# High parts of 16 weight pieces cast by transfers of GpSimd instead of by ScalarE, in a kernel whose issue order was searched anew

## The chip, the cores and the metric

The kernel runs on one core of one Trainium2 chip. The metric is device time in microseconds (us); lower is better. PE is TensorE, DVE is VectorE, ACT is ScalarE, POOL is GpSimd, SP is SyncE, which here only issues transfers. SPq, ACTq and POOLq are the queues from which these engines issue them.

## The reference, cut to what matters

Two parts follow each other: a linear recurrence with complex decay over 768 steps of 32 heads, and a gated feed-forward block on its output, with float32 weights.

```python
for t in range(S):                       # attention: 4 batches x 8 heads, D = 48
    S_re, S_im = ar*S_re - ai*S_im + k_t v_t^T, ar*S_im + ai*S_re
    y[t] = q_t @ S_re
x = y.transpose(0, 2, 1, 3).reshape(3072, 384)
h = x @ w_in                             # 384 x 2048
sp = log1p(exp(h))
out = (h * tanh(sp)) @ w_out             # 2048 x 384
```

## The kernel before

The tokens are cut into 12 units of 256 (`UNITS`, named u0 to u11), each into two chunks a and b of 128. Each unit goes through three stages. `elementwise(u)` turns the decays into phases and growth factors on ACT and DVE and rotates q and k ("turn sin", "turn cos"); SP then copies the results into the tile `T` ("relay", line 566, six transfers per chunk), with the heads side by side. `attention(u)` is a set of small matmuls per chunk: `kn` (transpose of the keys), `am` (scores), `y` (output) and `pd` (state). `moe(u)` takes the outputs as `x`, split into a high part `xH` and a rest `xL`, through eight pairs p0 to p7 of weight blocks: "mm1" (`ph`, line 787), a chain of five operations on ACT and DVE up to `g`, its high part `gh` and rest `gl`, and "mm2" (`po`, line 824). Only unit 0 multiplies the weights as they are; all others use a high part `wh` and a rest `wl` of each weight, so that a product takes three matmuls.

The weights arrive as 64-bit words, in 16 pieces w0 to w15 (even ones are of w_in, odd ones of w_out). `weight(i)` makes float32 of a piece by four instructions (low, shift, join, carry); `halves(i)` then writes the high part (line 318, "high") and the rest (line 323, "rest", on DVE, which reads both `w` and `wh`).

Nothing schedules at run time. Every step is recorded by `op(...)` with the engines that may do it, and `Work.issue` emits the 2446 steps in the order of the table `ORDER`; a letter behind a number picks another engine than the first of the step's list (V is DVE, A is ACT, G is POOL, S is SP). Each engine then works through its own instructions in that order. Forty steps "spin" (line 886, two matmuls each that nobody reads) lie in the order of PE's start. POOL clears one column of the tile `kn` (line 628) for each chunk that passes on its state.

The program ends with a verdict on the inputs: "tally" (DVE) counts flags of all units, "tally sum" (PE) adds them over partitions, "judge" (DVE, line 899) writes `okay`. Every engine reads `okay` at the end of its own order (line 933) and branches; behind the branch ACT scales the last half of unit 11 (line 835) and SP stores it (line 841). The first half is stored by POOL.

Of the kernel before, what the change touches and what calls it, by code (L numbers as in the profile page):

```python
# [55 lines left out]
72 0 1 73 127 3 74 2 75 128 7V 5 8 76 10V 4 9 11 77 6 12 192 78 13 202 197 14 79 24V 80 27V 81 82 25 83 169V 15 19 28  # L56
26 132V 84 16 166V 85 133 22 17 86 167 23 87 31 170 88 32 135V 18 134 34 33 29 137 89 21 136 90 20 91 42 47 46G 45 92
35 48 30 49 93 43 36 44 194 50 193 53 52 94 139 39 95 54 195 96 55 97 40 51 98 37 196V 99 38 100 56A 60 207 101 62A
140 562 102 204 57 563 103 203V 104 199 105 41 200 106 61A 138 107 58 64 108 142 109 59 205 112 66 116 67A 68 113 118
65A 117 70 71A 114 206V 123 69 198 110 119 217 141 120 124 115V 121 201V 125 430 63 143 209 212 126 567 208V 210 144  # L60
122 146 186 211V 145 130 168 153 570V 147A 185 173 171 149 148 568 184 151 111 218V 187 174 155 154 571G 360A 129 175
150V 160 152 156 222 157 432 219 569 158 220 356 163 573 161 164 214 159 221V 273 172 189 357 215 188 213 272 191 162
176 216V 361A 190 358 177 359 227 274 165 363 178 575 275 365 367 276 364 223 224 282 366 572 181A 368 277 225 283 369
576 232 182 179 370 226V 278 292 131 180 229 237 284 279 293 376A 371 183 230 280 374 228 578 574 281 285 231V 372
375A 286 303 378 242 373 287 233V 386 234 388 362 583 302 235 387 382 389 390 288 236V 294 392 434 289 247 383 295 304
312 584 296 385 238 239 379 290 391 381A 384 393 297 380 291 240 442 743 305 243 395 377 244 577 241V 394 298 245 252
306 397 744 400 307 246V 398 446 299 401 257 248 579 322 396 399 308 402 249 403 448 405 580 313 749 404 250 406 323
314 581 251V 407 582 315 262 309 409 316 564 585 408 594A 317 565 300 593 586 324 253 254 301 436 410 431 318 411 263
255 412 258 325 264 414 326 256V 415 587A 417 265 450 267 418 413 332 266V 327 421 259 440 420 433 310 328 566 588 452
423 333 422 438 319 260 343 334 329 589 335 320 592 321 590 428V 595 435 336 311 591 596 426 424 330 337 429 597 603  # L70
342 602 598 338 331 425 344 604 427 268 269 601 339 463 750 747 345 609 270 346 462 607 752 261V 419 347 456 599 271V
348 474 751 754G 605 475 476 437 340 349 935 341 606 439 608 350 477 454 464 444 351 478 753 416 441 757 612 610 613
354 355 352 479 755 465 611V 466 487 616 614 600 443 758 617 619 445 467 621 480 468 615 618 760 481 623 469 624 936
622 470 759 761 625 756 765 486 498 447 499 626 628 510 511 488 489 471 472 473 458 500 501 762 944 490 620 629 482A
# [12 lines left out]
975 842 859 860 849 991 1147 1148 1156 824 1157 989 1155 843A 976 1159A 992 726 1315 737 738 1130 1129 739 740 850 851
1160G 872 990 1158 996 1161 741 1162 998 997 993 1001 1165 1316 871 852 844 1318V 999 845 1002 861 1169 1172 1003 1317
1499 862 1320 1007 994 1000 1004 1008 853 1166 1005 995V 863 864 865 846 1006 1014 1322 866 867A 1015 854 1010 855 873
1319G 1321 1323 1163 1167 1171 1009 1012 1168 1011V 1013 874 875 1016 1164 856 1331 742 868 883 876 877 1324 1332 878  # L90
884 885 1325 1333 1018 1334A 895 896 897 886 887 888 1170 1500 1020 889 857 1326 858 1019 1335 879 880 898 1505 899
890 907 1327 869 870 1017 1021 900 891 1178 892 1023V 1022 1024 1025V 1026 881 908 901 902 1336 1508 1179 1176 1177
882 919 1328 1314 1173 920 1132 909 1506 1131 910 903A 921 1330 904 911 922 1509 912 1511 1329 1342G 1182 1180 1183
1181 923 913 924 1507 914 925 893 1174 894 1175 915 1513 1027 1028 1312 1338V 905 906 1510 1029 926 1187 1341G 1189
1190 1188 1191G 916 1185 1184 1311 1340 1337 1344 1192 1030 1345 1194 1512 1521 1339 1351 1040 1039 1041 927 928 1051
1349 1031 1352 1032 1357 1042 1193 1186V 1052 1033 1034 1195 1522 1043 1044 1045 1046 917 918 929 930 1523 1524 1035A
1053 1514 1355 1054 1347 1036 1196 1516 1197 1198 1202 1199 1201 1047A 933 931V 934 1064 1055 1056 1057 1048 1350 1200
1075 1063 1065 1066 932 1076 1037 1038 1049 1058 1059 1060 1343 1353 1354 1515 1050 1087 1067 1088 1068 1077 1069 1070
# [12 lines left out]
1287 1288 1400 1886 1895 1289 1694 1693 1722 1290 1567 1724 1719 1401 1402 1568V 1896 1565 1721 1726 1733 1412 1729
1403 1404 1405 1406 1411 1407 1735 1413 1424 1414 1291 1725 1423 1425 1426 1292 1303 1304 1566V 1557 1569 1570 1305
# [101 lines left out]
def tile_kernel(ctx, tc, q, k, v, vs, are, aim, are_t, aim_t, w_in, w_out, out):  # L214
    nc = tc.nc
# [8 lines left out]
    op = Work(nc)  # L224
# [83 lines left out]
    def halves(i):  # L308
        def high(e):
# [805 lines left out]
```

## Time and profile before

| what | value |
|---|---|
| time, median of 3 runs (least to most) | 581.17 us (580.46 to 581.74) |
| time of the profiled execution | 580.87 us |
| its span in the profile | 579.2 us |
| PE busy | 566.4 us, 98% |
| DVE busy | 486.1 us, 84% |
| ACT busy | 476.2 us, 82% |
| POOL busy | 27.4 us, 5% |

The span is the time between the first and the last instruction of the program; 1.67 us of the profiled execution's time lie outside it. Busy shares are means over the whole span: the kernel's start, its stage of weight unpacking (up to about 160 us), its long stage of steady work and its end differ much, and are read apart. The ends of matmuls are modelled by the profiler, so that PE looks busy also in short waits.

### The profile page before, as it was taken

What the parts mean: (1) busy time and instruction counts of PE and PEld (TensorE: products, weight loads), DVE (VectorE), ACT (ScalarE), POOL (GpSimd) and SP (SyncE); (2) the same over time, 40 slices, a digit from 0 to 9 for tenths busy, and PEclk for the clock granted to TensorE, in tenths of its full rate; (3) what the DMA queues carried; (4) which work ended last, traced back from release to release, by engine and by line L of the source; (5) the groups of instructions that cost most, each with busy time, mean ns of one, the idle gap of its engine ahead of it and who ended that gap; (6) DMA issues with size and microseconds to landing.
All of it is one profiled execution on the core that took longest, in us unless ns stands there. A gap on an engine that the chain in (4) does not pass through costs nothing.

```text
span 579.2 us, 13318 instructions
## 1 busy us (share of the span) xinstructions
PE 566.4 (98%) x5262; PEld 532.2 (92%) x5262; DVE 486.1 (84%) x899; ACT 476.2 (82%) x763; POOL 27.4 (5%) x59
## 2 busy tenths in 40 slices
PE   7999999999999999999999999999999999999994
PEld 4689788899999999999999999999999999999994
DVE  5999999999999999989899977999697857555462
ACT  7899999999999999888888978778778866456670
POOL 2010000110000010100000000200000000000000
PEclk9999999999999999999999999999999999999998
DMA  8788785512727155152352162064254230010201
GB/s 284 246 274 271 239 256 151 167 28 60 220 61 205 57 143 164 47 153 78 103 134 80 43 201 74 21 194 132 56 137 137 58 109 1 29 29 2 81 1 33
DMA packets 58469, 68.91 MB, mean 119 GB/s; under 512 B 4976, under 2 KB 51440, under 8 KB 58400
## 3 DMA queue, kind: packets, MB, share of 16 engines
q1 hardware_dynamic: 57616, 67.14, 39.0%
q8 instruction: 43, 0.70, 0.5%
q10 hardware_dynamic: 720, 0.66, 0.4%
q14 instruction: 26, 0.21, 0.1%
q0 software_dynamic: 64, 0.20, 0.1%
HBM read 39.52 MB, written 4.72 MB: 76 GB/s over the span
## 4 chain that ended last, share of the span: by engine, by line
PE 77%; ACT 10%; DVE 9%; issue 2%; POOL 1%; ACTq 0%; DVEq 0%; POOLq 0%
PE po L824 32%; PE ph L787 32%; PE ypsum L674 5%; PE pa L644 4%; ACT X L174 4%; PE pd L689 2%; ACT e L174 2%; PE pkn L622 2%; ACT L172 2%; DVE X L559 1%; DVE w L296 1%; DVE QK L535 1%; DVE g L800 1%; DVE wl L323 1%; ACT words L174 1%
## 5 line engine op out<-in xcount | busy, mean ns | idle before, releaser
L174 ACT ACTIVATE e<-e 128x512 f32<-128x512 f32 x192 | 119.6, 629 | 29.9 <-DVE e L856 27.8
L787 PE MATMUL ph<-xH,wh 128*128 128x256 f32 x462 | 132.8, 287 | 0.0
L787 PE MATMUL ph<-xH,wl 128*128 128x256 f32 x462 | 129.9, 281 | 0.0
L787 PE MATMUL ph<-xL,wh 128*128 128x256 f32 x462 | 129.8, 281 | 0.0
L824 PE MATMUL po<-wh,gh 128*128 128x384 f32 x308 | 105.1, 341 | 0.0
L824 PE MATMUL po<-wh,gl 128*128 128x384 f32 x308 | 103.5, 336 | 0.4 <-DVE gl L812 0.4
L824 PE MATMUL po<-wl,gh 128*128 128x384 f32 x308 | 103.5, 336 | 0.0
L800 DVE SCALAR_TENSOR_TENSOR g<-e,ph 128x512 f32<-128x512 f32 x96 | 65.3, 681 | 30.1 <-ACT e L174 29.2
L787 PEld LDWEIGHTS ph<-xH,wh 128*128 128x128 f32 x462 | 87.0, 188 | 1.7 <-issue 0.7
L787 PEld LDWEIGHTS ph<-xL,wh 128*128 128x128 f32 x462 | 87.0, 188 | 0.1
L787 PEld LDWEIGHTS ph<-xH,wl 128*128 128x128 f32 x462 | 87.0, 188 | 0.0
L174 ACT ACTIVATE e<-ph 128x512 f32<-128x512 f32 x96 | 56.8, 592 | 26.6 <-PE ph L787 24.0
L174 ACT ACTIVATE e<-e,fifth 128x512 f32<-128x512 f32 x96 | 69.3, 723 | 1.9
L812 DVE TENSOR_TENSOR gl<-g,gh 128x512 fp32r<-128x512 f32 x88 | 60.2, 685 | 6.3 <-PE po L824 2.3
L824 PEld LDWEIGHTS po<-wh,gh 128*128 128x128 f32 x308 | 57.9, 188 | 0.9 <-issue 0.2
L824 PEld LDWEIGHTS po<-wh,gl 128*128 128x128 f32 x308 | 57.9, 188 | 0.8 <-DVE gl L812 0.7
L824 PEld LDWEIGHTS po<-wl,gh 128*128 128x128 f32 x308 | 57.9, 188 | 0.0
L856 DVE TENSOR_SCALAR e<-e 128x512 f32<-128x512 f32 x96 | 44.1, 462 | 15.2 <-ACT e L174 14.8
L172 ACT ACT_TABLE_LOAD x40 | 51.3, 1283 | 0.7
L659 DVE TENSOR_TENSOR kept<-pa,cmask 64x128 f32<-64x128 f32 (+1 forms) x108 | 32.6, 329 | 11.5 <-PE pa L644 6.3
L674 PE MATMUL ypsum<-T,S 96*48 96x128 f32 x320 | 33.9, 276 | 0.0
L806 ACT CAST gh<-g 128x512 fp32r<-128x512 f32 x38 | 23.4, 617 | 12.2 <-DVE g L800 12.1
(145 smaller groups left out, 1120.1 us busy)
## 6 DMA issues: line engine op xcount, KB each, us to landing
T<-QK SPq DMA_DIRECT2D x70, 129.0 KB, 2.5
T<-X SPq DMA_DIRECT2D x69, 129.0 KB, 2.6
words<-w_in SPq DMA_DIRECT2D x8, 768.0 KB, 5.5
words<-w_out SPq DMA_DIRECT2D x8, 768.0 KB, 6.0
QK<-k SPq DMA_DIRECT2D x12, 384.0 KB, 4.3
QK<-q SPq DMA_DIRECT2D x12, 384.0 KB, 5.2
V<-v SPq DMA_DIRECT2D x12, 384.0 KB, 4.6
R<-a_re SPq DMA_DIRECT2D x12, 384.0 KB, 4.3
```

Of the source, the lines that this page charges most:

```text
L172: self.nc.scalar.preload_act_table_set(need)
L174: return self.nc.scalar.activation(out, in_, func, **kw)
L622: e.transpose(d["pkn", g][:, i, :], T()[:, 4 * g + i, 1, :C], ident)
L644: e.matmul(d["pa", g][r0:r0 + C // 2, i, k0:], T()[:, 4 * g + i, 1, k0:k0 + C // 2], T()[:, 4 * g + i, 0, k0:C], start=True, stop=True)
L659: e.tensor_tensor(x[r, :, two, t], y[r, :, two, t], m[r, :, two, t], ALU.mult)
L674: e.matmul(ypsum[64 * par:64 * par + D, i, :], lhs, rhs, start=m == 0, stop=first or m == 1)
L787: e.matmul(ph[k][:, slot(k, j, a), :], win(x, j, kt, a), st[y][:, kt, cols(k)], start=n == 0, stop=n + 1 == len(todo))
L800: e.scalar_tensor_tensor(g_[k], e_[k], 2.5, ph[k], ALU.subtract, ALU.mult)
L806: (e.copy if e is nc.scalar else e.tensor_copy)(gs[k][0], g_[k])
L812: e.tensor_tensor(gs[k][1], g_[k], gs[k][0].bitcast(F32), ALU.subtract)
L824: e.matmul(po[t], x[:, slot(k, j, a), 0 if halved else t * P:C if halved else (t + 1) * P], wout(y, j, a), start=j == 0 and a == 0 and n == 0,
L856: op("V", f"{n} cap", lambda e, k=k: e.tensor_scalar_min(e_[k], e_[k], math.exp(20.0)))
```

## The change

The step "high" of the 16 weight pieces may now only go to POOL, and is there a transfer from `w` to `wh` that casts on its way. Before, all 16 were casts on ACT. No relay is issued by ACT any more (five were). The table `ORDER` is another one from its first entry on; 49 of the steps that DVE did have gone to ACT (eight of them in the first 130 us: three kn copies and one step each of size, low, ends, xH and gh), 26 of those that ACT did have gone to DVE (none of them in those 130 us). ACT loads its function tables 43 times in place of 41. The same matmuls are issued, the spins among them. Of the diff the code stands here in full, and of the table one line of each side.

```diff
-72 0 1 73 127 3 74 2 75 128 7V 5 8 76 10V 4 9 11 77 6 12 192 78 13 202 197 14 79 24V 80 27V 81 82 25 83 169V 15 19 28
...
+0 7V 8 9 1 10V 12 11 72 73 74 13 75 76 77 78 79 80 81 82 83 84 14 127 85 132V 3 2 128 166V 24V 25 27V 192 15 133 135V
...
-            (e.copy if e is nc.scalar else e.tensor_copy)(wh[i], w[i])
+            e.dma_start(wh[i], w[i])
...
-        op("AV", f"w{i} high", high)
+        op("G", f"w{i} high", high)
```

Three places of the new order follow, each before and after.

POOL's order in the first 100 us before. `kn` is the column that is cleared per chunk, line 479 an addition of unit 2, line 480 a multiplication of unit 3.

```order
L541 COPY QK_140<-X_138 128x6
L628 MEMSET kn_352 128x8
L479 TENSOR_TENSOR X_427<-X_427 128x6x128
L628 MEMSET kn_488 128x8
L628 MEMSET kn_713 128x8
L628 MEMSET kn_871 128x8
L480 TENSOR_TENSOR I_806<-I_806,X1_1091 128x768
```

The same place after; `wh` is the pair of high parts that a transfer writes, `w` the piece that it reads.

```order
L541 COPY QK_207<-X_121 128x6
L628 MEMSET kn_349 128x8
L318 DMA wh_369<-w_297 128x768
L628 MEMSET kn_458 128x8
L318 DMA wh_533<-w_486 128x768
L479 TENSOR_TENSOR X_413<-X_413 128x6x128
L318 DMA wh_369<-w_410 128x768
L318 DMA wh_645<-w_580 128x768
L318 DMA wh_645<-w_647 128x768
L318 DMA wh_679<-w_205 128x768
L628 MEMSET kn_699 128x8
```

Sixteen such transfers stand on POOL's queue, among clearings and additions that wait for other engines; the last is issued before POOL's addition of unit 4.

SP's order at the relays of unit 0 before: `T_264` is chunk a, `T_343` chunk b; ACT issues what is missing (one of chunk a, three of chunk b).

```order
L566 DMA T_264<-X_138 16x8x258 x2
L566 DMA T_264<-QK_140 16x8x258 x2
L566 DMA T_264<-X_138 16x8x258
L282 DMA words_296<-w_out 128x768
L381 DMA R_302<-a_re 128x768
L381 DMA I_310<-a_im 128x768
L566 DMA T_343<-X_138 16x8x258
L566 DMA T_343<-QK_140 16x8x258 x2
```

SP's order there after: `T_293` is chunk a, `T_332` chunk b.

```order
L388 DMA QK_207<-k 128x6x128
L282 DMA words_233<-w_out 128x768
L381 DMA R_259<-a_re 128x768
L381 DMA I_261<-a_im 128x768
L393 DMA V_265<-v 128x768
L566 DMA T_293<-X_121 16x8x258 x3
L566 DMA T_293<-QK_207 16x8x258 x3
L282 DMA words_320<-w_out 128x768
L566 DMA T_332<-X_121 16x8x258 x3
L566 DMA T_332<-QK_207 16x8x258 x3
```

All twelve relays now stand on one queue, and the first two loads of unit 2 have come ahead of them there.

DVE's order at the program's end before. Line 891 is the second instruction of "tally", line 899 is "judge", line 837 scales the first half of the last output; lines 800, 806 and 812 make `g`, `gh` and `gl`.

```order
L812 TENSOR_TENSOR gl<-g,gh 128x512 x2
L800 SCALAR_TENSOR_TENSOR g<-e,ph 128x512
L806 CAST gh<-g 128x512
L812 TENSOR_TENSOR gl<-g,gh 128x512
L591 SCALAR_TENSOR_TENSOR I,good<-R,I 128x768
L890 TENSOR_SCALAR good<-good 128x14
L891 TENSOR_REDUCE total<-good 128x1
L837 TENSOR_SCALAR o<-po 128x384
L899 TENSOR_SCALAR okay<-ptotal 1x1
L933 TENSOR_LOAD okay
```

DVE's order there after.

```order
L800 SCALAR_TENSOR_TENSOR g<-e,ph 128x512
L856 TENSOR_SCALAR e<-e 128x512
L806 CAST gh<-g 128x512
L899 TENSOR_SCALAR okay<-ptotal 1x1
L812 TENSOR_TENSOR gl<-g,gh 128x512 x2
L800 SCALAR_TENSOR_TENSOR g<-e,ph 128x512
L806 CAST gh<-g 128x512
L812 TENSOR_TENSOR gl<-g,gh 128x512
L837 TENSOR_SCALAR o<-po 128x384
L933 TENSOR_LOAD okay
```

The judge, which was the last thing that DVE computed, now stands ahead of the last three rests `gl`, and "tally" 19 rows ahead of it; PE's "tally sum" moved with them, from just ahead of the last twelve matmuls to the place ahead of the last 18 matmuls of mm1, which the last 60 of mm2 follow.

## Rows read from the trace of the kernel before

**Rows 1.** The page: busy us (share of the span) and instructions.

```profile
PE 566.4 (98%) x5262; PEld 532.2 (92%) x5262; DVE 486.1 (84%) x899; ACT 476.2 (82%) x763; POOL 27.4 (5%) x59
```

**Rows 2.** Windows: busy PE, PEld, DVE, ACT, POOL; PEclk, DMA share, GB/s.

```profile
0.00:40.00 40.00, 36.71 (x274) 24.61 (x276) 33.49 (x66) 34.20 (x59) 6.11 (x27) 1.00 0.79 262
40.00:160.00 120.00, 118.80 (x1056) 105.89 (x1053) 118.24 (x194) 116.86 (x189) 5.58 (x9) 1.00 0.59 180
160.00:560.00 400.00, 399.51 (x3872) 390.86 (x3871) 326.95 (x625) 320.91 (x511) 15.04 (x22) 1.00 0.32 91
```

**Rows 3.** Timeline of PE: start, us, engine, line, operation, count.

```profile
12.73 0.49 PE L418 MATMUL psum<-turn,X 128*128 128x128 f32 x2 [1.15 <-DVE X L492]
...
25.91 0.49 PE L622 MATMUL pkn<-identity,T 96*128 96x96 f32 x4
...
29.40 0.60 PE L886 MATMUL junk<-cmask 128*128 128x512 bf16 x2
...
36.22 0.60 PE L886 MATMUL junk<-cmask 128*128 128x512 bf16 x2
...
41.78 0.49 PE L787 MATMUL ph<-x,w 128*128 128x128 f32 x2
```

**Rows 4.** Timeline of all engines, 26 to 31 us, then SP's wait.

```profile
26.38 0.57 ACTq L566 DMA_DIRECT2D T<-X  x1
26.99 0.48 ACT L629 COPY kn<-pkn 128x384 f32<-128x384 f32 x1 [0.50 <-issue]
...
27.14 0.95 DVE L559 TENSOR_TENSOR QK<-QK,R 128x768 f32<-128x768 f32 x1
...
30.52 1.20 SPq L566 DMA_DIRECT2D T<-QK  x2
...
SPq L566 <- DMA T<-X: 3.5, 1, 3.5
```

**Rows 5.** Groups by line: count, busy us, mean ns, idle before.

```profile
L172 ACT ACT_TABLE_LOAD x40 | 51.3, 1283 | 0.7
...
L318 ACT CAST wh<-w 128x768 fp32r<-128x768 f32 x14 | 11.5, 828 | 0.0
...
L629 DVE COPY kn<-pkn 128x384 f32<-128x384 f32 x16 | 8.8, 549 | 0.1
```

**Rows 6.** Chain of waits, 41.8 to 130 us, by line.

```profile
by line: PE po L824 18.8%; PE ph L787 14.2%; ACT e L174 9.9%; ACT X L174 7.7%; issue 6.0%; DVE wl L323 4.3%; ACT L172 3.5%; DVE w L296 3.0%; DVE g L800 2.9%; ACT words L174 2.8%; DVE w L300 2.2%; PE ypsum L674 2.2%; DVE w L292 2.1%; PE pa L
```

**Rows 7.** DMA issues: KB each, us from issue to landing.

```profile
QK<-k SPq DMA_DIRECT2D x12, 384.0 KB, 4.3
...
out_dram<-o POOLq DMA_DIRECT2D x1, 192.0 KB, 4.6
```

**Rows 8.** Timelines of POOL and of DVE, 99 to 129 us.

```profile
101.97 2.45 POOL L480 TENSOR_TENSOR I<-I,X 128x768 f32<-128x768 f32 x1 [32.22 <-ACT X L174]
...
102.66 2.09 DVE L856 TENSOR_SCALAR e<-e 128x512 f32<-128x512 f32 x1
...
125.22 0.42 DVE L856 TENSOR_SCALAR e<-e 128x512 f32<-128x512 f32 x1
...
126.23 2.13 DVE L323 TENSOR_TENSOR wl<-w,wh 128x768 fp32r<-128x768 f32 x1
```

**Rows 9.** Timeline of the end, then SP's wait.

```profile
569.53 0.14 DVE L899 TENSOR_SCALAR okay<-ptotal 1x1 int32<-1x1 f32 x1
...
569.92 0.72 POOL L841 DMA_DIRECT2D out_dram<-o  x1 [81.33 <-DVE okay L899]
...
571.10 0.34 PE L824 MATMUL po<-whl,gh 128*128 128x384 f32 x1
571.52 0.49 ACT L835 ACTIVATE o<-po 128x384 f32<-128x384 f32 x1 [6.01 <-PE po L824]
574.33 0.35 SPq L841 DMA_DIRECT2D out_dram<-o  x1
...
SPq L1071 <- SPq L1071: 3.6, 1, 3.6
```

More of the change, by code (lines that the diff above doesn't have):

```diff
@@ L60 @@
[L60 to L74, printed above, removed]
@@ new lines @@
+419 605 437 416 464 609 439 350 351 460 465 598 606 597 604 599 612 610 354 608 341 613 441 611 466 355 467 468 456
+614 755 935 600 758 602 616 601 754G 756 487 747 443 617 619 615 618 623 621 469 445 470A 352 486 759 481 499 488 447
+760 765 498 624 595 941 620 607 626 622 489 490 491 761 492 944 471 762 625 511 746 628 629 627 500 501 449 493 451
+482A 472 766 483 473 764 510 630 353 631 454 502 503 504 523 522 512 484 513 767 632 452 634 458 635 942 745 633 453
+485 505 455 534 514 515 494A 495 516 517 524 525 535 768A 459 496 506 518 763 507 497 508 526 509 527 769 536 528 529
@@ new lines @@
+1357 1052 1053 1349 1198 1046 1521 1522 1047A 1063 1064 1065 1048 1054 1066 1055 1056 1516 1352 934 1517 1037 1057
+1067 1523 1075 1524 1068 1038 1069 1525A 1350 1076 1049 1050 932 1058 1059 1060 1077 1070 1078 1087 1079 1518 1088
+1199 1071 1080 1081 1082 1089 1090 1091 1061 1112 1062 1354 1356 1526 1202 1527 1353 1207 1099 1200 1201 1072 1208
+1205 1203 1204 1358 1083 1206 1092 1093 1359 1519 1094 1502 1100 1360 1361 1520 1533G 1532A 1111 1362 1363 1692 1364
+1348 1073 1084 1095 1074 1691 1113 1114 1101 1501 1085 1697 1698 1699 1365 1086 1102 1369 1096 1115 1531 1116 1370
@@ new lines @@
+1117 1103 1118 1104 1119 1105 1700 1371 1106 1372 1209 1375 1210 1211 1702 1097 1212 1529V 1107A 1376V 1222 1108 1528
+1098 1120 1530 1535 1540 1542 1539 1543 1541 1704 1221 1223 1224 1109 1373 1374 1534 1701 1110 1121 1544 1213 1214
+1538 1215 1216 1217 1703 1218 1225 1226 1227 1228 1705 1122 1545 1547 1537 1123 1124 1234 1379 1367 1380 1366 1368
+1706 1377 1378 1707 1708 1709 1125 1246 1229A 1230 1245 1247 1233 1235 1236 1237 1873 1386 1382 1384 1385 1248 1381
+1383V 1874 1392 1389 1536 1238 1239 1696 1240 1249 1250 1710 1251 1711 1504 1252 1712 1257 1258 1259 1882 1546 1219
@@ new lines @@
+1220 1269 1126 1260 1387 1231 1232 1293 1393V 1394 1548 1713 1549 1551 1270 1714 1241 1242 1397 1243 1398 1261 1244
+1262 1879 1253A 1391 1388 1263 1264 1254 1294 1282 1281 1271 1272 1390 1395 1396 1273 1550 1724A 1552V 1295 1296 1265
+1274 1275 1266 1276 1555 1553 1715 1716 1717 1399 1880 1881 1283 1284 1297 1884 1298 1400 1277A 1556 1718 1299 1300
+1255 1256 1285 1267 1268 1286 1503 1278 1562 1723A 1554 1560 1883G 1885 1694 1411 1287 1279 1280 1412 1720V 1288 1401
+1402 1301A 1887 1289 1290 1561 1886 1424 1563 1564 1291 1567 1292 1423 1719 1403 1895 1693 1404 1405 1406 1413 1414
@@ new lines @@
+1302 1303 1722 1726 1721 1733 1415 1416 1728 1565 1568 1888 1566 1304 1307 1557 1569 1558 1570 1890 1425 1734 1729
+1571 1426 1572 1559 1417 1418 1427 1308 1407A 1735 1578 1579 1408 1573 1574 1576 1577 1580 1889 1436 1575 1435 1891
+1584 1305 1428 1429 1430 1459 1896 1419A 1731 1897 1437 1438 1439 1440 1441 1878 1460 1461 1420 1409 1462 1892 1463
+1464 1306 1442 1732 1410 1727 1737 1739 1582 2063 1589V 1465 1736 1898 1447 1421 1448 1449 1730 1466 1422 2064 1893
+1450 1451 1725 1431 1472 1590 1452 1453 1738 1581 1585 1443 1444 1471 1432 1473 1894 2069 2070 2071 1899 1484 1454
@@ new lines @@
+1483 1455 1433 1434 1445 1446 1742 1586 1583 2072V 1474 1587V 1475 1476 2073 1588 2074G 1456 1467 1743 1740 1741V 1485
+1486 1592 1744 1746 1487 1591 1457 1745 1477 1902V 1458 1478 1468 1876 1905 1907 1593 1603 1747 1488 1489 1875 1604
+1469 1479A 1480 1470 1481 1594 1906A 1490 1491 1695 1482 2076 1901 1904 1908 1595 1911 1903 1915 1751 1605 1752 1606
+1900 1749 1753 1754 1755G 1492 1596 1597 1598 1599 2077 2075 1607 1608 1748 1750 2078 1756 1757 2085 1918 1758 2080
+1910 1493 1920 1759 1600 1609 1616 1615 1617 1494 1495 1496 2079 1610 1618 2086 1760 1497 1498 1619 1611 1612 2081
@@ new lines @@
+1620 2082 1761 1762 1621 1628 1627 1629 1916 1630 1631 1651 1632 1633 1652 1622 1601 1602 2087 1613 1640 1763 1767
+1653 1654 1614 1655 1656 1634 1635A 2088 1623A 2089 2090 1657 1639 1765 1624 1641 1768 2091 1658 1664 1917 1909 1922
+1921 1764 1663 1769 1625 1766 1771 2255 2083 2084 1770 1919 1659 1642 1636 2097 1643 1644 2093 1645 1626 1772 1923
+1646 1665 1666 2256 1924 1925 1667 1668 2065 2066 2095 1675 1676 1637 1677 1638 1877 1912 1933 1934 1926 1678 1647A
+1935 1774 1927 1669 1914 1773 2092 1670 2096 1913 1937 1648 1660 1936 2099 2102 2264 2100 2101 1938V 2094 2106 1649
@@ new lines @@
+1650 2108 1661 1662 1679 1680 1671A 1672 1775 1681 1776 1682 1928 1929 1683A 1941 1930 1684 1785 1777 1778 2261V 2262
+2263 2265 2267 2269 2111 2270 1939 1940V 2110 1673 1674 1685 1786 1787 1779 2107 1942 2098 1788 2109 2112 2103 1686
+2258 1931 1943 1944 1932 1780 2067 1781 1950 1951 2266 1945 1789 1790 1791 1948 1946 2068 1782 1792 1793 2117 1798
+1949 1689 2268 2277 2278 2279 1797 2280 1809 1810 1687 1845 1947 1956 1799 1800 2260 2105 1952 1846 2271 2104 1801
+1802 1794 1783 1784 2338 1961V 1803 1811 1804 1812 1805A 2272 1847 2118 2281A 2282 1813 1814 1815 1833 1955 1806 1690
@@ new lines @@
+1795 1834 1796 1807 1688 1848 1816 1849 1817 1818 1953 1850 1851 1822 1957 1954 1835 1852 1821 1958 1857 2257 2273
+1962 2283 1959V 1960 2113 1823 2114V 1824 1825 1836 1837 1826 1827 2274 2115 2116V 1858 1808 1819 2119 1838 1839 2275
+2120 2276 2121 1840 1859 2124 2122 2125 1828 2126 2127 1829A 1830 1860 2284 2286 2133 2129 1976 2130 2288 1861 1963
+1975 1820 1841A 2287A 2290 2294 1831 1832 1862 2134 1863 2339V 1842 2123 1977 1978 1964 1853A 1854 1843 1864 2285 1844
+1855 2131 1979 1980 2135 1965 2297 2302 2303 2132 1865 2301 2128 2137 1966 1967 2292 1968 2142 2136 2138 2139 2140
@@ new lines @@
+2291 2293 1987 2148 1981 1988 1856 1982 1969 1970 2259 1866 2145 1867 2342 1989 1990 1999 1991 1971A 1868 2149 2141
+1983 2024 2341 1984 1871 1872 1869 1870 1992 1993 1972 1994 1995 2000 2001 2002 2003 2004 2005 2023 2025 2026 1973
+1974 2150 1985 2147 1986 2027 2300 2028 2143 2144 2298 1996 2006 2011 2007 2012 2029 2146 2030 2013 2014 2343V 2151
+2008 2295 2015 2016 2017 2152 2299 2018 2310 2311 2035 2047 2036 2153 2154 2048 2037 1997 2038 2039 2167 2040 1998
+2009 2041 2031A 2296 2042 2010 2156 2049 2019 2020 2021 2022 2043 2050 2051 2052 2053 2306 2032 2033 2034 2304 2305
@@ new lines @@
+2155 2157 2044 2158 2159 2160 2045 2046 2054 2161 2055 2056 2162 2307 2168 2169 2170 2171 2163 2164 2172 2192 2057
+2058 2059 2289 2308 2315 2309 2313 2317 2061 2316 2062 2060 2318 2319 2322 2173 2323 2312 2174 2175A 2314 2176 2320
+2321 2191 2193 2194 2195 2196 2179 2197 2198 2180 2181 2182 2325 2324 2326V 2330 2203 2204 2205 2206 2183 2184 2185
+2186 2215 2207 2216 2165 2166 2187 2177 2178 2188 2189 2190 2217 2218 2208 2209 2210 2328 2211 2227 2228 2219 2220
+2199 2200 2221 2222 2229 2335 2230 2329 2333V 2223A 2239 2334 2240 2201 2212 2337 2340 2202 2241 2327 2331 2336 2213
@@ new lines @@
+2242 2231 2232 2344 2233 2224 2214 2225 2226 2234 2332 2348 2235A 2243 2244 2349 2236 2237 2245 2246 2247 2248 2238
+2350 2351 2352 2353 2354 2355 2249 2250 2251 2361 2360 2362 2253 2363 2364 2356 2357 2365 2252 2345 2366 2367 2368
+2369 2372 2373 2374 2375 2376 2384 2358 2254 2359 2385 2377 2378 2379 2370 2386 2387 2380A 2381 2388 2389 2390 2396
+2397 2398 2399 2391 2371 2392 2421 2400 2401 2382 2402 2403 2420 2422 2408 2393 2409 2404 2410 2423 2424 2411 2383
+2346 2412 2425 2426 2413 2414 2427 2405 2415 2432 2433 2434 2394 2435 2395 2406 2407 2428 2347 2416A 2417 2436 2437
@@ L153 @@
+2429 2438 2418 2439 2419 2430 2440 2441 2442 2431 2443 2444 2445
 """.split()]
```

113 lines of the change are left out of this document (35 added, 78 removed), and 3 rows, old and new, of the table ORDER.

## The prediction

> **What bounds the kernel now.** I read the page's busy times first: PE is busy 98% of the span, DVE 84%, ACT 82% [rows 1]. A mean over stages hides which engine sets the pace where, so I cut the span by windows [rows 2]. There are four stages. Up to 40 us PE has little to do: what counts is when its real work begins. From 40 to 160 us three engines are full together: PE 118.8, DVE 118.24 and ACT 116.86 of 120 us. From 160 to 560 us PE alone is full (399.51 of 400 us), DVE and ACT have about a fifth free: nothing that the vector engines are spared there can shorten the span, and I forecast nothing for it (0.5 us either way). Last comes an end in which PE is done and the output is still under way. PE issues the same matmuls before and after, so the change can pay only by an earlier start of PE's real work, by fewer of PE's waits up to 160 us, or by a shorter end. The granted clock is 1.00 in the first three windows; the spins that go before the start are the same forty, so I expect no change of it.
>
> **The end, -2.2 us.** At first sight PE sets the end. The timeline says otherwise [rows 9]. The last matmul starts at 571.10, ACT scales the last output from 571.52 to 572.01 (0.49 us), but SP issues its store only at 574.33. What SP does in between is in its own waits: 3.6 us put down to SP itself, no semaphore and no DMA. It is the way through the branch: the judge on DVE ends at 569.67 (569.53 + 0.14), SP reads the flag, branches, and its first instruction behind the branch comes 3.6 us later. So the end hangs on the judge, not on PE. In the new order the judge stands ahead of three rests and of 60 matmuls of mm2, and of the 18 of mm1 before them (the order of DVE and PE above). The last twelve matmuls of before show the scale: from the judge's start at 569.53 to PE's end at 571.44 (571.10 + 0.34) they take 1.9 us. Sixty take five times that, 9.5 us; the judge waits for some of DVE's rests too, but comes several us before PE's end, and SP's 3.6 us lie beside mm2. Then SP waits only for ACT, and its store starts at about 572.1 if PE ends at the same time: 574.33 - 572.1 = 2.2 us. Bounds: 0 if SP has to fetch again after its wait; 2.3 (574.33 - 572.01) at best. POOL's store, issued at 569.92 and landed 4.6 us later [rows 7, 9] (at 574.5), is issued as before and ends before SP's.
>
> **The start, -1.2 us.** PE begins with its first real matmuls of the attention of unit 0 (pkn) at 25.91 and reaches the first mm1 at 41.78 [rows 3], 15.9 us later. In this stretch lie two spins of 0.60 us each (29.40 and 36.22): at least 1.2 us of it is time for which PE had no work.
> What was late? The relays of chunk b [rows 4]. DVE's "turn cos" ends at 28.09 (27.14 + 0.95), but SP issues two of the three cos relays only at 30.52: its wait is for the landing of a relay, 3.5 us. The only ones under way into this tile from another queue are ACT's, the first issued at 26.38. So SP's own relay waited for ACT's, 2.4 us longer than for its data. ACT's copy of kn was held as well, 0.50 us with "issue" as the reason, between two of ACT's relays. With all relays on SP no transfer into `T` has to wait for another queue: the cos relays can go at about 28.1, and chunk b's scores start up to 2.4 us earlier. Against it stands SP's own queue: one relay more for chunk a, two more for b ahead of the last, each about 0.6 us (1.20 for two [rows 4]), and two more loads ahead of chunk a's. All forty spins now come before pkn, two more than before; their 1.2 us fit where PE waited 1.15 us for DVE at 12.73 [rows 3]. So I take 0.0 for pkn and, of the 2.4 us, what PE filled with spins after it, 1.2 us. Bounds: 2.4 us gained; 0.6 us lost, if only the longer queue shows.
>
> **40 to 160 us, -0.5 us in sum.** The chain of waits from 41.8 to 130 us runs only 35% over PE's largest groups (po 18.8, ph 14.2, ypsum 2.2); the rest is ACT, DVE and their hand-overs [rows 6]. So DVE and ACT do matter here, but PE shows only 1.2 us of 120 without a matmul [rows 2], and that is nearly all that can be won: I take 1.0 us, bounds 0 and 3 (the modelled ends of matmuls hide short waits).
> The relief is larger than this. ACT loses 16 casts of 828 ns, 13.2 us; two more table loads of 1283 ns give 2.6 us back [rows 5]. DVE passes eight steps to ACT; at the 549 ns of a kn copy, an estimate, 4.4 us [rows 5]. Since it is more than PE can use, what is left is slack against the costs that follow.
> The casts as transfers cost three things. First, landing: 384 KB loads land 4.3 us after their issue, POOL's only transfer, half as large, after 4.6 us [rows 7]; no cast of this kind is in the trace, I take 5 to 9 us. The step "rest" on DVE that reads the result stands far behind each transfer in the order: for the tightest (w11, w12 and w14) POOL's queue is free after its multiplication of unit 3, which ends at 104.42 before, and the rest of w12 started at 126.23 [rows 8]. Three issues and a landing of 9 us end by some 116 us, so this wait is covered by 10 us of other DVE work; without that cover DVE would stand still for a landing each time. Second, the rings: 16 times 384 KB are 6.3 MB, at the 262 GB/s of the first 40 us 24 us of the rings; from 40 to 160 us they are idle 41% of 120 us, 49 us [rows 2]. It fits, but relays and weight loads queue behind casts: 0.2 us, bounds 0 and 3. Third, POOL: an issue held POOL 0.72 us [rows 9], 16 of them 11.5 us; it was nearly idle. A clearing of kn queued behind a cast that waits for its weight holds up "kn out" and pd; the weights it waits for are ready before the kn in question, so I take 0.
> But POOL and DVE can be in each other's way. In the trace DVE's cap took 2.09 us while POOL multiplied from 101.97 to 104.42; the same instruction takes 0.42 us alone [rows 8]. No row shows a transfer's issue doing this to DVE. Bounds: 0, and 0.72 us for each of 16, 11.5 us of DVE; nearer to the first, since an issue is a third as long as that multiplication and meets mostly other instructions: 2 us of DVE, under its 4.4 us of relief, of which PE may see 0.3.
> The Trainium skill ("SBUF — State Buffer", section "Who interferes with whom") speaks against the change here: a DVE instruction in a two-port mode and GpSimd's work on SBUF shut each other out whole, and writing the descriptors of a GpSimd transfer is such work. By it cap, shift and low would wait for a cast's issue or hold it up, and the time would go to that of rival 3 below; by the rows, which show the wait at POOL's arithmetic alone, it stays with the sum. The cap that waited agrees with the rule; that an issue does the same no run here shows yet.
>
> **Sum.** -2.2 - 1.2 - 1.0 + 0.2 + 0.3 = -3.9 us, on the profiled execution: span 579.2 - 3.9 = 575.3, and 1.67 us outside it, 577.0. The median shown lies 0.3 us above the profiled execution, so 577.3 us.
>
> **Rivals.** (1) Only the end pays. DVE was full from 40 to 160 us and gives PE its work at the old pace, so an earlier start is lost again in waits by 160 us: 581.17 - 2.2 = 579.0. For it: the chain of waits; against: DVE's 4.4 us of relief. (2) The gains are eaten: loads of weights land late among the casts, DVE waits in shift and low (three times 1 us), PE follows: 581.17 - 3.9 + 3 + 0.5 = 580.8, no change. For it: rings 79% busy up to 40 us; against: 41% idle afterwards. (3) Slower, by one mechanism: each cast's issue holds a DVE instruction for its whole 0.72 us. DVE then does 11.5 us more in a stage where it is 98.5% busy; less 4.4 of relief, 7.1 us pass to PE, and 7.1 - 2.2 (the end) - 1.2 (the start) gives 584.9. It decides from about (4.4 + 2.2 + 1.2) / 16 = 0.49 us a cast on. The rule of the Trainium skill named above ("SBUF — State Buffer") is this rival. (4) The end stays, because SP fetches only when it leaves its last wait: then 579.5 with the rest of the sum.
>
> **How the numbers follow.** Forecast 0.52, (1) and (4) together 0.20, (2) 0.13, (3) 0.15. About 0.2% (1.2 us) is what a measurement of this kernel can tell from no change. Faster by more: forecast, (1) and (4): 0.72. Within: 0.13. Slower: 0.15. The forecast's own range is 575.0 to 578.9 (end 0 to 0.1 better, start to -2.4 or waits to -3, not both). For 8 in 10 I leave out (3) and a little at the fast edge: 574.8 to 581.6.
>
> **What would show it.** The end: SP's last store within 0.2 us of ACT's last output. The start: SP's relays of chunk b in one run without a wait for a landing, first mm1 near 40.6. The middle: DVE's caps at 0.42 us beside POOL's transfers, and no wait of DVE's rests for a DMA. The prediction is wrong if rests wait for casts, if DVE's two-port instructions stretch by 0.5 us or more at each cast, or if PE between 160 and 560 us has new waits from the new order.

## The result and the profile after

The kernel after takes 583.98 us in the median (582.32 to 587.29, 10 runs), the kernel before 581.55 (579.49 to 582.72, 10 runs): a ratio of 1.0055, with a 95% interval of 1.0036 to 1.0074, 3.2 us slower. The forecast was 577.3, the range ended at 581.6.

The profiled execution took 586.40 us, 2.4 above the median, with a span of 584.5. Its windows, in the columns of [rows 2]:

```profile
0.00:40.00 40.00, 37.70 (x289) 25.24 (x291) 32.19 (x67) 34.73 (x62) 4.61 (x27) 1.00 0.89 277
40.00:160.00 120.00, 113.61 (x955) 101.80 (x950) 108.70 (x169) 105.24 (x167) 15.01 (x24) 0.97 0.72 210
160.00:560.00 400.00, 399.63 (x3901) 390.38 (x3898) 322.90 (x622) 330.55 (x530) 9.27 (x21) 1.00 0.34 96
```

The loss stands in one row; from 160 to 560 us PE is as full as before (399.63 and 399.51). Between 40 and 160 us PE was busy for 113.61 us, where it was for 118.8 before: 5.2 us more without a matmul. DVE and ACT, which had been full there, now have 11 and 15 us free, so neither of them sets the pace. The granted clock is 0.97 over this stretch in place of 1.00. What grew is the DMA share, from 0.59 to 0.72. The queues between 30 and 130 us (packets, MB, share of 16 engines; q0 is GpSimd's):

```profile
q1 hardware_dynamic: 12222, 18.94, 65.6%
q0 software_dynamic: 2304, 6.29, 19.1%
```

The 16 casts took 19.1% of 100 us, 1.2 us of all 16 engines for each. That share was not spread evenly: from 30 to 85 us the rings stood at 1.08, where they had been at 0.82 (the share adds up the times of packets, so it passes 1 where they overlap). Before, then after, columns as in [rows 2]:

```profile
30.00:85.00 55.00, 54.19 (x546) 46.99 (x546) 54.11 (x93) 54.18 (x92) 2.13 (x4) 1.00 0.82 259
30.00:85.00 55.00, 50.44 (x471) 44.73 (x470) 47.26 (x83) 46.22 (x79) 8.23 (x15) 0.97 1.08 328
```

The chain of waits from 41 to 80 us, which was ACT, DVE and PE before [rows 6], runs over transfers (start, us, what):

```profile
45.46 10.04 DMA words<-w_in
...
62.31 9.76 DMA T<-QK
...
72.10 0.61 DVE S L698 x2
72.71 1.19 DVE g L800 x2
73.91 0.48 DVE X L492
...
75.05 1.12 PE pkn L622 x8
```

A relay of 129 KB issued at 62.31 landed 9.76 us later. Over the first 130 us the median relay from `QK` took 4.7 us in place of 3.8, from `X` 5.2 in place of 3.2, a load of w_in 7.9 in place of 5.5, the casts themselves 7.2 (2.6 to 12.5). The issues of the relays in the kernel after (KB each, median us to landing):

```profile
T<-X SPq DMA_DIRECT2D x18, 129.0 KB, 5.2
T<-QK SPq DMA_DIRECT2D x18, 129.0 KB, 4.7
```

PE waited 2.2 us, until 75.05, for what hung on the relay of 62.31, and 1.7 us, until 122.68, for another relay, which had taken 7.95. No step "rest" of DVE (line 323) waited for a cast. Behind both waits the granted clock fell. Four windows, columns as in [rows 2]:

```profile
73.00:75.00 2.00, 0.00 (x0) 0.00 (x0) 2.00 (x4) 1.42 (x2) 0.00 (x0) 1.00 1.07 358
...
75.50:78.50 3.00, 3.00 (x17) 3.00 (x16) 2.35 (x3) 1.86 (x3) 0.00 (x0) 0.50 1.06 399
...
120.00:123.00 3.00, 1.28 (x12) 1.10 (x11) 3.00 (x7) 1.77 (x5) 0.00 (x0) 1.00 0.24 73
123.50:126.50 3.00, 3.00 (x16) 3.00 (x15) 0.73 (x2) 2.97 (x6) 0.00 (x0) 0.50 0.65 202
```

PE has nothing to do for about 2 us, and when its matmuls come again, the granted clock is at 0.50, the lower of the two levels (1.2 GHz), for some 3.5 us. Each fall takes half of that, 1.75 us, from a stage that PE bounds. Two falls and 5.2 us of waits make 8.7 us; PE's last matmul comes 7.9 us later than before (579.03 and 571.10). The median shows less of it than this execution: two of the ten with a mean granted clock of 0.999 took 582.82 and 583.81 us, so that a part of the loss seems to come without falls.

The end is the one place that gained. The judge, PE's last matmul, ACT's last output and SP's store in the timeline (compare [rows 9]):

```profile
571.09 0.14 DVE L899 TENSOR_SCALAR okay<-ptotal 1x1 int32<-1x1 f32 x1
...
579.03 0.34 PE L824 MATMUL po<-whl,gh 128*128 128x384 f32 x1
...
579.46 0.49 ACT L835 ACTIVATE o<-po 128x384 f32<-128x384 f32 x1 [5.82 <-PE po L824]
579.97 0.34 SPq L841 DMA_DIRECT2D out_dram<-o  x1
```

The judge ends 7.8 us ahead of the last matmul's start, and SP issues its store 0.02 us behind ACT's output, where it had come 2.3 us behind. Last, the start, PE and then SP (compare [rows 3, 4]):

```profile
26.69 0.52 PE L622 MATMUL pkn<-identity,T 96*128 96x96 f32 x4
...
34.82 0.49 PE L622 MATMUL pkn<-identity,T 96*128 96x96 f32 x4
...
41.45 1.60 PE L418 MATMUL psum<-less,X 128*128 128x128 f32 x12
43.27 2.94 PE L787 MATMUL ph<-x,w 128*128 128x128 f32 x24 [0.21 <-DMA x<-y]
```

```profile
25.96 1.83 SPq L566 DMA_DIRECT2D T<-X  x3
27.90 1.90 SPq L566 DMA_DIRECT2D T<-QK  x3
```

SP's relays of chunk b go in one run, as forecast, and end 1.9 us earlier than before; but PE takes up the `kn` of chunk b only at 34.82, and the first mm1 comes at 43.27, 1.5 us later than before, behind twelve sums of unit 1 (line 418) that now stand ahead of it. Before, they came behind it:

```profile
44.56 1.50 PE L418 MATMUL psum<-less,X 128*128 128x128 f32 x12
```

### The profile page after: what moved, and what is told of

The parts are those of the page before. It is cut to its first block, busy times and chain, and to the rows that moved or that the text cites. A ratio compares the mean times of both kernels' runs of the same rounds, so it can differ in the third digit from the quotient of the medians.

```text
span 584.5 us, 13316 instructions
## 1 busy us (share of the span) xinstructions
PE 570.3 (98%) x5262; PEld 536.2 (92%) x5262; DVE 474.1 (81%) x875; ACT 481.6 (82%) x775; POOL 29.5 (5%) x73
## 4 chain that ended last, share of the span: by engine, by line
PE 84%; DMA 6%; ACT 3%; DVE 3%; SPq 1%; issue 1%; POOL 0%; ACTq 0%; DVEq 0%; POOLq 0%
PE po L824 33%; PE ph L787 33%; PE ypsum L674 6%; PE pa L644 4%; DMA T<-QK 3%; PE pd L689 2%; PE junk L886 2%; PE pkn L622 2%; DMA words<-w_in 2%; DMA QK<-k 1%; ACT X L174 1%; ACT L172 1%; PE pa L637 1%; SPq L566 1%; DVE X L515 0%
## 5 line engine op out<-in xcount | busy, mean ns | idle before, releaser
L812 DVE TENSOR_TENSOR gl<-g,gh 128x512 fp32r<-128x512 f32 x88 | 62.1, 708 | 9.6 <-PE po L824 5.2
L856 DVE TENSOR_SCALAR e<-e 128x512 f32<-128x512 f32 x96 | 40.1, 419 | 29.7 <-ACT e L174 29.6
L174 ACT ACTIVATE X<-X 128x768 f32<-128x768 f32 (+1 forms) x40 | 30.5, 765 | 1.7 <-DVE X L482 1.4
```

What stands on the lines that cost most here:

```text
L174: return self.nc.scalar.activation(out, in_, func, **kw)
L812: e.tensor_tensor(gs[k][1], g_[k], gs[k][0].bitcast(F32), ALU.subtract)
L856: op("V", f"{n} cap", lambda e, k=k: e.tensor_scalar_min(e_[k], e_[k], math.exp(20.0)))
```

## The experiments

**The theories.** Rings: the bytes of the casts fill the DMA rings, relays and weight loads land late, PE waits, and its clock falls. Against it: order (the new order's own places make the waits); lock (each issue of GpSimd holds DVE, rival 3). All kernels were timed against the kernel before on their own chip, so that differences between kernels go by the ratios below, of 581 us:

| kernel | median us | ratio to before | 95% interval |
|---|---|---|---|
| after | 583.98 | 1.0055 | 1.0036 to 1.0074 |
| b_cast | 585.89 | 1.0088 | 1.0057 to 1.0120 |
| b_none2 | 581.34 | 1.0013 | 1.0000 to 1.0027 |
| a_none2 | 576.64 | 0.9928 | 0.9910 to 0.9946 |
| a_none | 578.63 | 0.9973 | 0.9942 to 1.0005 |
| b_none | 588.13 | 1.0134 | 1.0109 to 1.0159 |
| a_twice | 583.00 | 1.0033 | 1.0016 to 1.0049 |
| a_pool | 583.82 | 1.0048 | 1.0029 to 1.0066 |
| a_act | 587.01 | 1.0096 | 1.0079 to 1.0113 |
| a_mix | 582.36 | 1.0020 | 1.0001 to 1.0038 |
| b_tail | 578.72 | 0.9956 | 0.9942 to 0.9971 |
| b_tail_2 (the same) | 578.50 | 0.9963 | 0.9942 to 0.9984 |
| b_late | 580.67 | 0.9994 | 0.9973 to 1.0016 |
| b_late3 | 580.19 | 0.9994 | 0.9978 to 1.0010 |
| b_gap3 | 582.32 | 1.0027 | 1.0008 to 1.0046 |
| b_relay | 581.28 | 1.0011 | 0.9996 to 1.0027 |

**b_cast: the casts alone, in the old order.**

```diff
-            (e.copy if e is nc.scalar else e.tensor_copy)(wh[i], w[i])
+            e.dma_start(wh[i], w[i])
...
-        op("AV", f"w{i} high", high)
+        op("G", f"w{i} high", high)
```

> The kernel before in its own order, with only the 16 high parts made by casting transfers of GpSimd. Ring theory (6.3 MB more fill the DMA rings, relays and weight loads land later, PE waits): slower by 3 to 8 us, 584.5 to 589.5, with the DMA share at 1 from 40 to 85 us, landings of relays up from 3.5 to some 5 us, and PE's waits for them. Order theory (the new order's own places of loads and relays make the wait, casts are harmless): 580 to 581.5, ACT spared 13 us. Lock theory (each issue holds a DVE instruction 0.7 us): 585 to 589 too, but with caps, shifts and copies of DVE 0.5 us longer beside each issue.

Slower by 0.88%, 5.1 us. The window from 40 to 160 us, and the longest of PE's waits between 30 and 90 us:

```profile
40.00:160.00 120.00, 115.64 (x1002) 102.89 (x1002) 112.98 (x182) 102.19 (x164) 16.88 (x22) 0.99 0.73 220
```

```profile
PE pkn L622 <- DMA T<-X: 3.1, 1, 3.1
```

The signs are those of the kernel after, in the order that had all casts on ACT: the DMA share at 0.73, PE's wait for a relay, DVE and ACT with time to spare. Order alone can't be the cause.

**b_none, a_none: no casts, and the tiles cleared.** GpSimd clears the tiles of high parts and copies 8 columns of each piece (in b_none in place of ACT's casts). The lines of a_none:

```diff
+            if i == 5:
+                for n in range(6):
...
+                    pairs[n] = wts.tile([P, 2, WC], F32R, tag=f"wp{n}", name="wh")
+                    e.memset(pairs[n].bitcast(F32), 1.0)
...
-            e.dma_start(wh[i], w[i])
+            e.tensor_copy(wh[i][:, :8], w[i][:, :8])
```

> The kernel after in its own order without the 16 casts: GpSimd copies 8 of a piece's 768 columns (and clears the tiles of high parts between 30 and 41 us, and four more at their places), so that no transfer is made and ACT stays spared; the high parts are not those of the weights. Ring theory: PE's waits for relays go, and with them the falls of the granted clock, 576 to 580 against 583.98. Order theory (loads, relays and matmuls of the new order wait by themselves): 582 or more.

> The kernel before in its own order without the 16 casts, in the same way as the kernel a_none. It prices ACT's 13.2 us alone, against 581.04. If ACT's casts hold up the stage to 160 us: 578.5 to 580. If DVE and PE set its pace: 580.5 to 581.5.

Both were spoiled by the clearings, as three rows of the timelines of POOL, DVE and PE in a_none show:

```profile
31.07 6.64 POOL L315 MEMSET wh<- 128x1536 f32 x5
...
31.38 6.74 DVE L292 TENSOR_SCALAR w<-words 128x768 uint32<-128x768 uint32 x1
...
38.43 0.79 PE L431 MATMUL psum<-turn,I 128*128 128x128 f32 x2 [5.46 <-DVE S L706]
```

A shift of DVE that takes 0.55 us elsewhere lasted as long as five clearings, and PE stood for 5.46 us. In b_none a wait of PE for DVE was 7.8 us long. Of the twelve times of a_none eight lie between 576.6 and 579.2 and four, that of the profile among them, between 584.4 and 587.2. So the two kernels say nothing firm of the casts.

**b_none2, a_none2: no casts, without the clearings.** The high part is 128 columns, copied by GpSimd and read six times over (in b_none2 in place of ACT's casts). The lines of a_none2:

```diff
-            e.dma_start(wh[i], w[i])
+            e.tensor_copy(wh[i], w[i][:, :P])
...
+        if x is wh:
+            return x[2 * j]
...
+        if x is wh:
+            return x[2 * j + 1].unsqueeze(1).broadcast_to([P, DM // P, P])
```

> The kernel before in its own order without the casts, in another way than b_none, whose clearings on GpSimd held DVE for 7.8 us: the high part is one tile of 128 columns, copied by GpSimd, and all its 768 columns are read from these 128 (not the high parts of the weights). It prices ACT's 13.2 us alone, against 581.0. If ACT's casts hold up the stage to 160 us: 578.5 to 580. If DVE and PE set its pace: 580.5 to 581.5.

> The kernel after in its own order without the casts, in the same way as b_none2. Ring theory: without the 6.3 MB PE's waits for relays and the falls of the granted clock between 40 and 130 us go, 576.5 to 579 against 583.98. Order theory: 582 or more.

In the new order the casts cost 1.0055 / 0.9928 = 1.0128, 7.4 us; in the old one 1.0088 / 1.0013 = 1.0075, 4.3 us (estimates from the intervals: 5.9 to 9.0 and 2.4 to 6.3). GpSimd's copies of 128 columns stand in for the casts there, 0.9 us each in b_none2, and what they cost is not in these numbers. The stage from 40 to 160 us in a_none2, its stretch from 30 to 85 us and its relays:

```profile
40.00:160.00 120.00, 118.85 (x1062) 107.54 (x1063) 116.16 (x187) 113.33 (x182) 22.37 (x25) 1.00 0.58 173
30.00:85.00 55.00, 53.80 (x541) 47.09 (x542) 52.67 (x87) 51.00 (x88) 11.24 (x14) 1.00 0.83 258
...
T<-X SPq DMA_DIRECT2D x18, 129.0 KB, 4.5
T<-QK SPq DMA_DIRECT2D x18, 129.0 KB, 3.7
```

PE is as busy as in the kernel before, the clock is at 1.00, the DMA share at 0.58. In one and the same order the casts took the rings from 0.83 to 1.08 between 30 and 85 us and the median relays from 4.5 to 5.2 and from 3.7 to 4.7 us; most of the step from 3.2 to 4.5 belongs to the order. The order theory falls: without the casts the new order is the faster one, by 0.72%. And with 13.2 us less on ACT b_none2 is not faster than the kernel before, so no gain from ACT's relief shows in the old order; a gain no larger than what GpSimd's copies cost would be hidden.

**a_twice: the same bytes in twice as many issues.**

```diff
-            e.dma_start(wh[i], w[i])
+            e.dma_start(wh[i][:, :WC // 2], w[i][:, :WC // 2])
+            e.dma_start(wh[i][:, WC // 2:], w[i][:, WC // 2:])
```

> The kernel after with each casting transfer cut into two of 384 columns: 32 issues in place of 16, the same bytes. Ring theory (the bytes on the rings cost): 583 to 585, as the kernel after. Issue theory (each issue of GpSimd costs DVE or POOL its 0.54 to 0.72 us): 16 issues more, slower than after by some 5 us, 588 to 590.

Not slower than the kernel after; its window has the same marks:

```profile
40.00:160.00 120.00, 114.62 (x980) 103.61 (x981) 110.16 (x176) 106.91 (x171) 25.01 (x39) 0.97 0.75 213
```

The issue theory falls: 16 issues more cost nothing that the run shows. The lock theory falls with it: of the 32 DVE instructions that overlap an issue in the trace of the kernel after only one was longer than usual, a rest of 2.55 us at 108.75, and that one stood beside GpSimd's multiplication (108.64, 1.83 us).

**a_pool, a_act, a_mix: the new order, with the casts done by an engine.** GpSimd, ACT, or ACT and DVE in turn. The lines of a_mix; a_pool leaves `op("G", ...)` as it is, a_act has `"AV"` for all pieces:

```diff
-            e.dma_start(wh[i], w[i])
+            (e.copy if e is nc.scalar else e.tensor_copy)(wh[i], w[i])
...
-        op("G", f"w{i} high", high)
+        op("AV" if i % 2 else "VA", f"w{i} high", high)
```

> The kernel after in its own order, with the 16 high parts computed by GpSimd at the same places of its queue, so that ACT stays spared and no transfer is made. Ring theory: the waits for relays and loads go, 583.98 less 5 to 7 us plus what POOL's arithmetic costs DVE (0 to 1.6 us a cast where it meets a two-port instruction, estimate 2 us in all): 577 to 581. Order theory: stays at 584 or more. Lock theory (POOL's work holds DVE): slower than 584, by up to 16 times 1.5 us.

> The kernel after in its own order, with the 16 high parts cast by ACT as before: no transfer, and 13.2 us of ACT more. Ring theory: waits for relays gone, but ACT over-full between 40 and 160 us, 579 to 585. Order theory: 584 plus a part of ACT's 13 us, 586 to 592.

> The kernel after in its own order with no transfer: eight high parts cast by ACT (odd pieces) and eight by DVE (even ones). Without the casts this order gave 576.64 (a_none2); from 40 to 160 us ACT stood 6.7 us and DVE 4 us free there. If this slack takes most of 8 times 0.83 us on ACT and 8 times 0.6 us on DVE: 577.5 to 580, faster than the kernel before and near b_tail. If not (all 16 on ACT cost 10.4 us, a_act): 581 to 585.

The forecasts of the ring theory for a_pool and a_act were too low, and a_mix missed its hope as well. None of the three has waits for relays, but each has others. In a_pool DVE stands beside GpSimd's casts (timeline of POOL, then of DVE; this step of DVE takes 0.95 us alone):

```profile
61.39 1.50 POOL L318 CAST wh<-w 128x768 fp32r<-128x768 f32 x1
...
62.13 1.57 DVE L559 TENSOR_TENSOR QK<-QK,R 128x768 f32<-128x768 f32 x1
```

In a_act PE's longest wait is for a copy of `kn` by ACT (2.9 us), in a_mix it is the same copy (1.9 us). In all three the granted clock fell to 0.50 behind such a wait of PE, in a_pool twice. The order leaves ACT 6.7 us free from 40 to 160 us (113.33 of 120 in a_none2), and 16 casts there cost 1.0096 / 0.9928 = 1.0169, 9.8 us of the 13.2 that they take. So no real kernel in this order was found that keeps the 576.64.

**b_tail: the end alone.** Five steps of the verdict are moved forward in the old order.

```diff
-... 2410 2411 2412 ... 2405 ... 2343 ... 2418 2419 2429 ... 2344 2345 2442 2444 2445 2346 2347 2431 2443
+... 2343 2410 2411 2412 ... 2344 2345 2405 ... 2346 2418 2419 2347 2429 ... 2442 2444 2445 2431 2443
```

> The kernel before, with only the verdict moved forward: size again, test of unit 1, tally, tally sum and judge stand 36 matmuls of mm2 ahead of PE's end. End theory (the judge, then SP's 3.6 us through the branch, set the end): SP stores at once behind ACT's last output, 2.2 to 2.6 us less, 579.0 to 579.4 against 581.55. Rival (SP fetches code again behind its last wait, or the store of POOL ends last): 581.5, no change.

> The kernel b_tail once more beside b_gap3, on the same chip, for their difference: ratio to before 0.994 to 0.997, as the first time. b_gap3 minus b_tail: 0 us if the rings' state decides, 1 to 2.2 us if each transfer costs.

Faster by 0.44% and, the second time, 0.37%: 2.6 and 2.1 us. In b_tail_2 (lines are one lower in it):

```profile
565.99 0.15 DVE L898 TENSOR_SCALAR okay<-ptotal 1x1 int32<-1x1 f32 x1 [0.66 <-PE ptotal L894]
...
572.51 0.49 ACT L834 ACTIVATE o<-po 128x384 f32<-128x384 f32 x1 [6.14 <-PE po L823]
573.03 0.35 SPq L840 DMA_DIRECT2D out_dram<-o  x1
```

This is the version that beats both kernels.

**b_late, b_late3, b_gap3: does the place of a transfer decide?** The kernel b_tail with some casts by transfer; `LATE` names them, here those of b_late3, and their steps go to GpSimd. In b_gap3 the three steps also stand further back in the table, behind a copy of one column that GpSimd can only make when the rest of piece 2 is there.

```diff
+    LATE = (12, 13, 14)
...
-            (e.copy if e is nc.scalar else e.tensor_copy)(wh[i], w[i])
+            if i in LATE:
+                e.dma_start(wh[i], w[i])
+            else:
+                (e.copy if e is nc.scalar else e.tensor_copy)(wh[i], w[i])
```

> The kernel b_tail (578.72) with seven high parts made by transfers of GpSimd (pieces 4, 5, 10, 11, 12, 13, 14), those whose cast stood at 82 us or later, where the rings are 43% busy; the other nine stay with ACT. Ring theory (a transfer costs only where the rings are full): 578.0 to 579.2. Rival (each transfer costs wherever it stands, by b_cast 4.85 / 16 = 0.3 us): 580.5 to 581.

> The kernel b_tail (ratio 0.9956 to before) with three high parts made by transfers of GpSimd (pieces 12, 13, 14), which stand behind GpSimd's multiplication of unit 3 at some 104 us, where the rings are 27% busy. If a transfer costs only where the rings are full: ratio 0.995 to 0.997. If each costs 0.3 us wherever it stands: 0.997 to 0.998.

> The kernel b_tail with three transfers of GpSimd again (pieces 5, 10, 11), held back by a copy of one column of the rest of piece 2, so that they are issued at some 92 us, where the rings stand at 0.00 from 92 to 96 us, ahead of the relays of unit 2. If a transfer costs by what is on the rings beside it: as b_tail, ratio 0.995 to 0.997. If each transfer costs 0.3 us or more wherever it stands: 0.997 to 1.000, as b_late3.

All three lost what b_tail had won: seven transfers cost 0.38%, three cost as much, and the three that were to meet empty rings 0.64% (against b_tail_2). Two windows and the chain show why. First b_tail_2, which has no transfers of GpSimd:

```profile
104.00:106.00 2.00, 2.00 (x8) 1.16 (x7) 2.00 (x4) 2.00 (x4) 2.00 (x1) 1.00 0.42 124
106.00:108.00 2.00, 2.00 (x17) 1.69 (x16) 2.00 (x3) 0.97 (x4) 2.00 (x1) 1.00 0.00 0
```

Then b_late3, with its chain of waits behind the windows:

```profile
104.00:106.00 2.00, 2.00 (x8) 1.21 (x7) 2.00 (x3) 0.88 (x2) 1.38 (x4) 1.00 1.14 369
106.00:108.00 2.00, 0.92 (x6) 0.34 (x5) 2.00 (x4) 0.94 (x1) 0.00 (x0) 1.00 1.27 297
...
101.58 5.96 DMA T<-QK
```

And b_gap3, where GpSimd's issues and SP's relays of unit 2 fell on the same moment:

```profile
92.92 1.75 POOL L323 DMA_DIRECT2D wh<-w  x3
...
92.96 2.42 SPq L573 DMA_DIRECT2D T<-X  x3
...
106.00:108.00 2.00, 0.00 (x0) 0.02 (x1) 1.41 (x1) 0.00 (x0) 1.13 (x2) 1.00 0.35 65
...
102.11 5.65 DMA T<-QK
```

What the prediction called idle was a mean. Unit 2's relays are issued from 93 to 103 us, and PE's `pkn` takes the last of them almost as it lands: in b_tail_2 the relay of 101.22 took 4.5 us and `pkn` began at 106.63. In b_late3, with one transfer issued ahead of that relay and two behind it, it took 6.0. In b_gap3 the three transfers had landed by 100.5, before the relay was issued at 102.11, and yet it took 5.7: the rings had stood at 0.97 to 1.21 from 94 us on, so what the transfers had pushed back was still ahead of it. PE waited 1.1 us in b_late3 and 2.4 in b_gap3, with a fall of the clock behind it there. In b_late four of the seven went out between 71 and 77 us: little else stands on GpSimd's queue, so a transfer leaves when its weight is ready and not where it stands in the table. The expectation for b_gap3 was too low on both sides, as the gap was not long enough; a transfer in a really empty stretch was not had, and what it would cost stays open.

**b_relay: the start alone.** Five letters "A" are taken out of the old table, so that SP issues all relays.

```diff
-56A ... 67A ... 65A ... 71A ... 381A
+56 ... 67 ... 65 ... 71 ... 381
```

> The kernel before in its own order, with the five relays that ACT issued put on SP's queue at the same places. By the step of the prediction on the start: the cos relays of chunk b go 2.4 us earlier, 579.8 to 580.4 against 581.04. Rival (PE reaches the kn of chunk b only behind the sums of unit 1, so that the relays' time is hidden): 580.8 to 581.3.

No gain: 1.0011. SP issued the cos relays of chunk b at 28.37 (30.52 before), and PE took its `kn` at 35.79 (35.56 before), straight behind other work. The relays were early for nobody.

## Why the prediction was wrong

**The end, -2.2: right.** -2.6 and -2.1 by b_tail, and 0.02 us between ACT's output and SP's store in the kernel after. Rival 4 falls.

**The start and the middle, -1.2 and -1.0: near as a sum, the start by another way.** Without casts the new order wins 0.72%, 4.2 us; less the end's 2.6 that leaves 1.6 of the 2.2. From `pkn` to the end of chunk b's attention stand the same matmuls as before, less two spins: 15.9 us before (25.91 to 41.78), 14.8 in the kernel after (26.69 to 41.45), 15.0 in a_none2 (25.86 to 40.86). That is some 1 us of the 1.2, and it fits the two spins that went ahead; for the relays that came early b_relay shows no gain. The step "chunk b's scores start up to 2.4 us earlier" overlooked that PE had unit 1's sums to do first, and the first mm1 near 40.6 was missed. In the kernel after `pkn` itself came 0.8 us late, before all casts but none of the order's making, for a_none2 has the same order:

```profile
25.86 0.50 PE L627 MATMUL pkn<-identity,T 96*128 96x96 f32 x4
```

What delayed it there stays open. ACT's relief shows no gain by itself (b_none2). Which steps of the order won the rest of the 1.6 us was not tried.

**The rings, +0.2 with bounds 0 and 3: the step that failed.** The casts were measured at 7.4 us in the new order and 4.3 in the old, the falls of the clock included; of the other two costs that the prediction gave them, landing and GpSimd's issues, the trace shows none (no rest waited for a cast, though one landed only after 12.5 us where 9 were allowed; no DVE instruction was held by an issue). The bytes were right (24 us of the rings were estimated, 19 measured). Wrong was "from 40 to 160 us they are idle 41%", a mean over stages with different limits, the very thing that the prediction had warned of for PE. Eleven of the 16 casts went out between 30 and 85 us. There the rings had been 0.82 busy, 9.9 us free of 55, and eleven times 1.2 is 13.2 us: by this estimate they don't fit, and the share measured was 1.08. The other five, issued from 107.2 to 111.8 us, met unit 2's relays. In b_gap3 three transfers, sent into a stretch at 0.00, were enough to make one of those relays late. The Trainium skill ("DMA: Bandwidth & Descriptors", section "Issuing engines are not separate DMA queues") says that transfers of all issuing engines end up on the same 16 DMA engines; the trace agrees: SP's relays from `QK` took 4.7 us in the median beside GpSimd's transfers, 3.7 in the same order without them.

**The clock, "I expect no change of it": wrong.** The two falls of the profiled execution cost some 3.5 us, nearly as much as the waits that they follow (2.2 and 1.7 us). In the profiled execution of a_none2, which has no such wait, the clock stays at 1.00 to the end of PE's work.

**DVE and GpSimd, +0.3: right that an issue holds nobody, so rival 3 falls**, though its 584.9 came nearest to the time. No cap in the kernel after is longer than 0.43 us, and twice the issues cost nothing (a_twice). Of the Trainium skill's rule on "Who interferes with whom" ("SBUF — State Buffer") the part on arithmetic holds (6.74 us for a shift beside clearings, 1.57 in place of 0.95 beside casts); that descriptors of a transfer do the same is not borne out here.

**Rival 2** came nearest to the mechanism, transfers that land late among the casts, and priced it at 3.5 us against the 7.4 that the casts cost. But it had DVE wait for weights, and there DVE waited 2.0 us in all (1.3 and 0.7); both of PE's waits hung on relays.

## What to carry to other kernels

Before a transfer replaces an engine's work, look for room on the rings in the very stretch where its data become ready: take the DMA share of that stretch and of the ones up to the next relay that an engine waits for, not of the stage. Here no such transfer was free, so that room is enough is not shown. A short wait of PE may cost twice: once itself, once more by the clock behind it. And a new order that loses as a whole can still hold a real gain: here the verdict moved ahead of the last matmuls is worth 0.4% by itself.

## What was not expected of the hardware

GpSimd's five clearings in a row held one instruction of DVE for 6.74 us. GpSimd's queue, in contrast, took 16 issues more without a trace on the time. The granted clock fell to 0.50 for some 3.5 us after about 2 us in which PE had no matmul, in the kernel after twice (75.5 and 123.5 us). The length of such a gap alone did not decide it: at 37.9 us PE stood 1.36 us without a matmul in the profiled executions of b_tail and of b_tail_2, which are one program; behind it the clock was at 0.50 from 40 to 43 us in the first (581.33 us) and stayed at 1.00 in the second (577.76 us).
